# Gated mix of local attention and a spatial MLP: where w_sp is scaled, where wo is reordered, and when the late attention is issued

## The chip, the cores and the metric

The kernel runs on one core of one Trainium2 chip. A core has five engines that run their own queues of instructions: TensorE (PE, matrix products into PSUM, which has eight banks of 512 float32 columns), VectorE (DVE), ScalarE (ACT), GpSimd (POOL) and SyncE (SP). SP issues every DMA of this kernel. An engine takes its instructions strictly in order, so one that waits holds up all behind it. The metric is the device time in microseconds (us) of one execution; lower is better.

## The reference

There is one input x of 2048 rows (S) by 1024 columns (D). Two branches are computed from it and mixed by a gate per row:

```python
# A: 32 heads of 32; each position attends to 8 positions, 0, 2, 4, ... 14 back
q, k, v = split(x @ wqkv)
o = softmax(q . k[pos - 2*w] * 32**-0.5, over w = 0..7) @ v[pos - 2*w]
a = o @ wo
# B: gated MLP with a product over the positions
z = gelu(x @ w_in)                    # 2048 x 3584
z1 = z[:, :1792]
z2 = layernorm(z[:, 1792:])
g = w_sp @ z2 + b_sp[:, None]         # w_sp is 2048 x 2048
b = (z1 * g) @ w_out
# mix
s = sigmoid((x * gate_w).sum(-1))
out = s * a + (1 - s) * b
```

All inputs and the output are bfloat16.

## The kernel before, in words

Almost all of SBUF is one tile, `arena`, cut by hand into regions that are used again by later stages (`Z_OFF`, `X_OFF`, `A_OFF`, `CD_OFF`, `EF_OFF`). The instructions are written in a fixed order. A class `Beat` sets it: it counts an assumed time of TensorE (`beat.run`), and work of other engines is put into their queues when its due time in that count has come (`beat.at` for single calls, `beat.steps` for the chain of DVE work of attention). Due times decide only the order within each queue; the hardware then runs each queue as its waits allow.

The stages on TensorE, with their lines:

1. *Column chunk 0 of z2* (L274, first 128 products): x is loaded transposed, then 448 columns of the right half of `x @ w_in` are computed and passed through gelu.
2. *q/k/v* (L531): eight head groups (g) of 16 tiles; ACT copies each tile out of PSUM (L534), SP stores it to memory in three DMAs per four tiles (L540 to L542), and loads it back in another layout for attention. Attention of groups 0 to 5 runs on DVE from here on (`attention_steps`): key products (L293, L296, L299), softmax (L304 to L318, the exponential on ACT at L311), value products (L326, L332, L333, L329).
3. *The rest of z2* (L274, 384 products): gelu, sums of squares on ACT (L553), mean and variance in `stats`, normalisation to float16 in `norm`.
4. *z1* (L579): 14 column tiles f of the left half, four products of 512 rows each. ACT applies gelu (L581) into one of two slots `z1s`, and SP stores the slot to memory (L583). A slot is free again when its store has landed. All four tiles of an f, and those of the next f, find PSUM banks: there are eight.
5. *The product over positions* (L588): `g_group`, for four quarters q of the rows of w_sp and seven column pairs j. It is a Strassen-Winograd scheme with seven products instead of eight, with sums of w_sp blocks (`s_sums`) and of z2 blocks (`t_sums`) on DVE.
6. *The product with w_out* (L659): 16 row tiles in the order 8 to 15, 0 to 7; ACT scales the result into `mix` (L661). Attention of groups 6 and 7 runs on DVE beside it (`late_steps`).
7. *The product with wo* (L678, L683, L692): o, which attention stored to memory in `o_d`, is read back transposed. `combine` (L667) adds the two branches on DVE into one of three output slots, and SP stores it (L671).

Because w_sp is small in value, each of its rows is scaled by a power of two before it becomes float16. `scale_pair` does this in stage 2 for two blocks of 128 rows at a time: it loads them (L406), sums absolute values on ACT (L409), forms the power on DVE (L413, L414), scales on ACT (L419) and stores float16 rows to memory (`wsc_d`, L423). `load_half` (L445) later reads these back with transposing DMAs, four per quarter. The bias is scaled alike (`bias_scaled`), stored as `bt_d` element by element (L561) and read back broadcast to all partitions (L563). `load_wo` (L396) loads wo with a row order that fits the layout of o, by four DMAs whose destination takes every fourth partition. `load_oT_first` (L399) reads six of the eight groups of o for four row tiles; the rest (L388) and the other twelve whole row tiles (L390) are read after the late attention has stored its part (L344).

Of the kernel before, what the change touches and what calls it, by code (L numbers as in the profile page):

```python
# [11 lines left out]
BF = mybir.dt.bfloat16  # L12
# [3 lines left out]
P = 128  # L16
S = 2048
# [24 lines left out]
G_EARLY = 6  # L42
EXPO = 0x7F800000
# [14 lines left out]
def kernel(  # L58
# [31 lines left out]
    wsc_d = dpool.tile([S, S], F16, name="wsc_d")  # L90
    bt_d = dpool.tile([S], BF, name="bt_d")
    o_d = dpool.tile([S, D], BF, name="o_d")
# [33 lines left out]
    bt_n = sm.tile([P, 16], BF, name="bt_n")  # L126
    cm05 = sm.tile([P, 16], F32, name="cm05")
# [19 lines left out]
    junk = reg(EF_OFF + 3 * WGS, FH)  # L147
    w1_slots = [reg(EF_OFF + o, KT * n).rearrange("p (k c) -> p k c", k=KT)
                for o, n in ((0, 512), (4096, 512), (0, 512), (12288, 256))]
    z1s_slots = [reg(EF_OFF + 8192 + r * 2048, 2048).rearrange("p (c t) -> p c t", c=4) for r in range(2)]  # L150

    def z2_room(r, dt):
        v = reg(Z_OFF, 16 * FH) if dt is BF else reg(Z_OFF, 16 * FH).bitcast(dt)
        return v.rearrange("p (i f) -> p i f", i=16)[:, 2 * r:2 * r + 2, ZC:ZC + 1024]

    nat_slots = [z2_room(r, BF) for r in range(4)]
    sc_slots = [z2_room(4 + r, F16) for r in range(3)]
    abs_junk = z2_room(7, BF)
# [7 lines left out]
    class Half:  # L166
        def __init__(self, off):
            v = [reg(off + 2048 * r, 2048).bitcast(F16).rearrange("p (k t) -> p k t", k=8) for r in range(7)]
            both = reg(off, 8192).bitcast(F16).rearrange("p (h i t) -> p h i t", h=2, i=16)
            self.rows = [both[:, 0], both[:, 1]]  # L170
# [4 lines left out]
    y_slots = [reg(EF_OFF + r * 7168, 7168).rearrange("p (f t) -> p f t", f=NF) for r in range(2)]  # L175
    bt_bc = reg(CD_OFF + 14336, S)
    snaps = [[reg(CD_OFF + 16384 + (3 * r + n) * 512, 512).bitcast(F32) for n in range(3)] for r in range(2)]
    u3 = reg(A_OFF + 21504, 512).bitcast(F32)
    gb_slots = [reg(X_OFF + 14336 + r * 1024, 1024).rearrange("p (f t) -> p f t", f=2) for r in range(2)]

    w_out_sb = reg(CD_OFF, NF * D).rearrange("p (f n) -> p f n", f=NF)
    y_back = [reg(Z_OFF + r * 7168, 7168).rearrange("p (f t) -> p f t", f=NF) for r in range(2)]
    mix = [reg(o, 2048).bitcast(F32) for o in [Z_OFF + 14336 + 2048 * r for r in range(7)]
           + [X_OFF + 2048 * r for r in range(8)] + [EF_OFF + 8192]]
    wo_sb = reg(EF_OFF, KT * D).rearrange("p (k n) -> p k n", k=KT)
    ob_slots = [reg(CD_OFF + 16384 + r * 1024, 1024) for r in range(3)]
    oT_first = [reg(EF_OFF + 10240 + r * 768, 768).rearrange("p (k t) -> p k t", k=6) for r in range(4)]
    oT_rest = [reg(EF_OFF + 13312 + r * 256, 256).rearrange("p (k t) -> p k t", k=2) for r in range(4)]
    oT_whole = [reg(A_OFF + r * 1024, 1024).rearrange("p (k t) -> p k t", k=KT) for r in range(12)]
# [156 lines left out]
    def attention_steps(g0, g1, t):  # L346
        beat.at(t - 8.0, lambda: load_qk(g0))
        beat.at(t - 7.9, lambda: load_v(g0))
        for g in range(g0, g1):
# [7 lines left out]
            beat.at(t + (1.0 if g == g0 else 5.0), soft_exp)  # L357
# [40 lines left out]
    def load_oT_first(n):  # L398
        sync.dma_start_transpose(oT_first[n], o_d[n * P:(n + 1) * P, 0:6 * C])  # L399

    def scale_pair(n, t):
        a = 2 * n

        def load():
            for r in range(2):
                sync.dma_start(nat_slots[2 * (n % 2) + r], wsp_v[a + r])  # L406

        def norm1(r):
            nc.scalar.activation(abs_junk, nat_slots[2 * (n % 2) + r], ACT.Abs, accum_out=l1[:, a + r:a + r + 1])  # L409

        def power():
            sl = slice(a, a + 2)
            nc.vector.tensor_scalar(l1[:, sl], l1[:, sl], 2.0 ** -30, 2.0 ** -11, ALU.max, ALU.mult)  # L413
            nc.vector.tensor_scalar(rs[:, sl].bitcast(U32), l1[:, sl].bitcast(U32), EXPO, EXPO,  # L414
                                    ALU.bitwise_and, ALU.bitwise_xor)
            beat.on_vector(0.4)

        def scale(r):
            nc.scalar.activation(sc_slots[(2 * n + r) % 3], nat_slots[2 * (n % 2) + r], ACT.Copy,  # L419
                                 scale=rs[:, a + r:a + r + 1])  # L420

        def store(r):
            sync.dma_start(wsc_d[(a + r) * P:(a + r + 1) * P, :].rearrange("t (n s) -> t n s", n=2),  # L423
                           sc_slots[(2 * n + r) % 3])

        beat.at(t, load)
        beat.at(t + 6.0, lambda: norm1(0))
        beat.at(t + 8.5, lambda: norm1(1))
        beat.at(t + 11.0, power)
        beat.at(t + 17.0, lambda: scale(0))  # L430
        beat.at(t + 19.5, lambda: scale(1))
        beat.at(t + 20.0, lambda: store(0))
        beat.at(t + 22.5, lambda: store(1))

# [6 lines left out]
    def load_half(q):  # L441
        for h in range(2):
            for r in range(2):
                a = 4 * q + 2 * r + h
                sync.dma_start_transpose(halves[q % 2].rows[h][:, :, r * P:(r + 1) * P], wsc_d[a * P:(a + 1) * P, :])  # L445
# [73 lines left out]
    for n in range(8):  # L519
        scale_pair(n, beat.now + 14.0 + 16.5 * n)  # L520
# [28 lines left out]
    load_w1(1)  # L549
    for i in range(16):  # L550
        for c in range(1, 4):
            z2_tile(i, c)
        nc.scalar.activation(junk, z2[:, i, :], ACT.Square, accum_out=s2[:, i:i + 1])  # L553
        if i % 4 == 3:
            beat.at(beat.now + 6.0, lambda i=i: stats(i))
            for ii in range(i - 3, i + 1):
                beat.at(beat.now + 11.0, lambda ii=ii: norm(ii))
    beat.at(beat.now + 8.0, gates)
    beat.at(beat.now + 9.0, bias_scaled)
    bt_v = bass.AP(tensor=bt_d.tensor, offset=bt_d.offset, ap=[[1, P], [P, 16], [1, 1]])  # L560
    beat.at(beat.now + 14.0, lambda: sync.dma_start(bt_v, bt_n[:].rearrange("p (a o) -> p a o", o=1)))  # L561
    beat.at(beat.now + 24.0, lambda: load_half(0))
    beat.at(beat.now + 50.0, lambda: sync.dma_start(  # L563
        bt_bc, bass.AP(tensor=bt_d.tensor, offset=bt_d.offset, ap=[[0, P], [1, S]])))

    for f in range(NF):
        ch = f // 4
        w1 = w1_slots[ch]
        if f == 4:
            load_w1(2)  # L570
        if f == 6:
            load_w1(3)
# [3 lines left out]
        for c in range(4):  # L576
# [5 lines left out]
            beat.run(KT * 512)  # L582
        sync.dma_start(z1_d[:, :, f * 512:(f + 1) * 512].rearrange("c p t -> p c t"), z1s)  # L583
# [43 lines left out]
    for q in range(NQ):  # L627
        if q < NQ - 1:
            beat.at(beat.now + 0.5, lambda q=q: load_half(q + 1))
        else:  # L630
            beat.at(beat.now + 0.5, lambda: sync.dma_start(w_out_sb, B_w_out.rearrange("(f p) n -> p f n", p=P)))
        if q == 0:
            beat.at(beat.now + 0.6, lambda: load_z1(1, 0, NF))
        elif q < NQ - 1:
            beat.at(beat.now + 3.0, lambda q=q: spill_y(q - 1))
            beat.at(beat.now + 16.0, lambda q=q: load_z1(q + 1, 0, NF))
        for j in range(NFL):
            g_group(q, j)
            if j == 4 and q < NQ - 1:
                for fn in s_sums(q + 1):  # L640
                    fn()

    beat.steps = late_steps(beat.now + 10.0)
    for r in range(2):
        beat.at(beat.now + 3.0, lambda r=r: unspill_y(r))
# [3 lines left out]
    for n, a in enumerate(order):  # L649
        q, r = a // 4, a % 4  # L650
        y = y_slots[q % 2] if q >= 2 else y_back[q]
        if n == 8:
            beat.at(beat.now + 1.0, load_wo)
            for m in range(4):
                beat.at(beat.now + 1.5, lambda m=m: load_oT_first(m))
# [9 lines left out]
    def combine(psa, a, c0, c1):  # L665
        ob = ob_slots[a % 3]
# [3 lines left out]
    def store(a, c0, c1):  # L670
        sync.dma_start(out2[a * P:(a + 1) * P, c0:c1], ob_slots[a % 3][:, c0:c1])  # L671

    first = {}
    for a in range(4):
        for c in range(2):
            first[a, c] = psum.tile([P, 512], F32, name="psa", tag="ps")
            for kt in range(6):
                nc.tensor.matmul(first[a, c][:], oT_first[a][:, kt, :], wo_sb[:, kt, 512 * c:512 * (c + 1)],  # L678
# [50 lines left out]
```

## Time and profile before

| What | us |
|---|---|
| Median of three runs (728.46 to 729.84) | 728.98 |
| The profiled execution: its own time | 731.04 |
| The profiled execution: its span in the trace | 729.3 |
| TensorE busy in the span | 697.0 |
| VectorE busy | 501.3 |
| ScalarE busy | 311.7 |
| First product of q/k/v, of the rest of z2, of z1 | 32.84, 207.34, 280.08 |
| First product over positions, with w_out | 382.56, 553.73 |
| Last product ends, by the timeline | 726.11 |

The page gives for each group of instructions its line, engine, operation, the tiles, the number of instructions, their total busy time and mean duration, and the idle time of the engine ahead of them with what ended it. The chain that ended last is TensorE for 73% of the span. A waiting instruction is put down to the engine or DMA that came last.

### The profile page before, as it was taken

What the parts mean: (1) busy time and instruction counts of PE and PEld (TensorE: products, weight loads), DVE (VectorE), ACT (ScalarE), POOL (GpSimd) and SP (SyncE); (2) the same over time, 40 slices, a digit from 0 to 9 for tenths busy, and PEclk for the clock granted to TensorE, in tenths of its full rate; (3) what the DMA queues carried; (4) which work ended last, traced back from release to release, by engine and by line L of the source; (5) the groups of instructions that cost most, each with busy time, mean ns of one, the idle gap of its engine ahead of it and who ended that gap; (6) DMA issues with size and microseconds to landing.
All of it is one profiled execution on the core that took longest, in us unless ns stands there. A gap on an engine that the chain in (4) does not pass through costs nothing.

```text
span 729.3 us, 10622 instructions
## 1 busy us (share of the span) xinstructions
PE 697.0 (96%) x4282; PEld 469.0 (64%) x4305; DVE 501.3 (69%) x556; ACT 311.7 (43%) x588; POOL 12.1 (2%) x23
## 2 busy tenths in 40 slices
PE   8999998999799999997999999999999999995698
PEld 4588887888665554443448888888886444442243
DVE  1003859999899999995964665757557764994153
ACT  4447779787768795324332222222221232210000
POOL 1000000000000121000000000000000000000000
PEclk9999999999999999999999999999999999997989
DMA  9989998999993204799449172360508206013932
GB/s 213 210 223 258 245 286 247 293 297 264 282 277 109 84 2 141 37 123 327 138 152 194 67 216 103 87 233 1 202 2 316 106 1 159 1 55 86 202 113 74
DMA packets 189520, 117.15 MB, mean 161 GB/s; under 512 B 147872, under 2 KB 171680, under 8 KB 188448
## 3 DMA queue, kind: packets, MB, share of 16 engines
q1 hardware_dynamic: 189472, 116.49, 58.9%
q8 instruction: 33, 0.54, 0.3%
q14 instruction: 15, 0.12, 0.0%
HBM read 60.30 MB, written 40.44 MB: 138 GB/s over the span
## 4 chain that ended last, share of the span: by engine, by line
PE 73%; DVE 9%; DMA 7%; SPq 5%; ACT 4%; issue 1%; DVEq 0%; ACTq 0%
PE ps L588 23%; PE ps L531 14%; PE ps L274 13%; PE ps L579 13%; PE psa L692 5%; PE psb L659 5%; DVE arena L326 2%; SPq L390 2%; DVE arena L293 2%; DMA arena<-in_B_w_sp_dram 1%; DVE arena L296 1%; DVE arena L332 1%; ACT arena L534 1%; DMA arena<-k_d 1%; DMA arena<-in_A_wo_dram 1%
## 5 line engine op out<-in xcount | busy, mean ns | idle before, releaser
L531 PE MATMUL ps<-arena 128*128 128x384 bf16 x1024 | 168.5, 328 | 6.1 <-ACT arena L534 4.4
L588 PE MATMUL ps<-arena 128*128 128x256 f16 x1568 | 171.3, 273 | 0.0
L531 PEld LDWEIGHTS <-arena 128*128 128x128 bf16 x1024 | 147.8, 144 | 26.8 <-issue 7.9
L588 PEld LDWEIGHTS <-arena 128*128 128x128 f16 x1568 | 153.4, 98 | 18.0
L579 PE MATMUL ps<-arena 128*128 128x512 bf16 x439 | 98.2, 384 | 4.4 <-ACT arena L581 3.9
L274 PE MATMUL ps<-arena 128*128 128x448 bf16 (+1 forms) x512 | 97.4, 353 | 1.1 <-DMA arena<-in_B_w_in_dram 1.1
L659 PE MATMUL psb<-arena 128*128 128x512 bf16 x439 | 96.4, 379 | 0.5
L296 DVE TENSOR_TENSOR arena<-arena 128x4096 bf16<-128x4096 bf16 (+1 forms) x64 | 77.6, 1212 | 11.6 <-DMA arena<-in_A_wo_dram 9.7
L579 PEld LDWEIGHTS <-arena 128*128 128x128 bf16 x448 | 44.2, 99 | 58.2 <-issue 6.4
L274 PEld LDWEIGHTS <-arena 128*128 128x128 bf16 x512 | 50.0, 98 | 48.0 <-issue 1.6
L293 DVE TENSOR_TENSOR arena<-arena 128x8192 bf16<-128x8192 bf16 x16 | 70.8, 4422 | 11.1 <-DMA arena<-k_d 10.9
L659 PEld LDWEIGHTS <-arena 128*128 128x128 bf16 x448 | 43.8, 98 | 52.7
L326 DVE TENSOR_TENSOR arena<-arena,att_A 128x8192 bf16<-128x8192 bf16 x16 | 70.8, 4422 | 9.0 <-DMA arena<-v_d 8.7
L534 ACT CAST arena<-ps 128x384 bf16<-128x384 f32 x128 | 55.3, 495 | 23.6 <-PE ps L531 19.4
L581 ACT ACTIVATE arena<-ps 128x512 bf16<-128x512 f32 x56 | 32.2, 598 | 65.2 <-PE ps L579 40.3
L661 ACT ACTIVATE arena<-psb,omr 128x512 f32<-128x512 f32 x32 | 21.6, 687 | 72.2 <-PE psb L659 61.9
L667 DVE SCALAR_TENSOR_TENSOR arena<-psa,g_s,arena 128x512 bf16<-128x512 f32 (+2 forms) x33 | 23.4, 732 | 41.8 <-DMA out_dram<-arena 16.9
L692 PE MATMUL psa<-arena 128*128 128x512 bf16 (+2 forms) x197 | 44.3, 387 | 6.7 <-DVE arena L667 6.0
L606 ACT COPY arena<-ps 128x256 f32<-128x256 f32 x28 | 10.4, 372 | 84.5 <-PE ps L588 84.5
L276 ACT ACTIVATE arena<-ps 128x448 bf16<-128x448 f32 x64 | 34.3, 537 | 24.4 <-PE ps L274 23.9
L692 PEld LDWEIGHTS <-arena 128*128 128x128 bf16 x200 | 19.8, 101 | 31.6 <-issue 9.9
L615 DVE TENSOR_TENSOR arena<-ps,arena 128x256 f32<-128x256 f32 x28 | 11.9, 423 | 39.9 <-PE ps L588 39.7
(78 smaller groups left out, 479.3 us busy)
## 6 DMA issues: line engine op xcount, KB each, us to landing
arena<-z_d SPq DMA_DIRECT2D x5, 1792.0 KB, 7.5
arena<-in_B_w_sp_dram SPq DMA_DIRECT2D x16, 512.0 KB, 5.6
wsc_d<-arena SPq DMA_DIRECT2D x16, 512.0 KB, 5.6
arena<-k_d SPq DMA_DIRECT2D x8, 960.0 KB, 7.0
arena<-v_d SPq DMA_DIRECT2D x8, 960.0 KB, 7.1
z_d<-arena SPq DMA_DIRECT2D x14, 512.0 KB, 3.4
arena<-in_A_wqkv_dram SPq DMA_DIRECT2D x24, 256.0 KB, 4.7
q_d<-arena SPq DMA_DIRECT2D x32, 128.0 KB, 4.4
```

The source lines that it names most:

```text
L274: nc.tensor.matmul(ps[:, 0:N], xT[:, kt, i * P:(i + 1) * P], w2[:, kt, ZC * c:ZC * c + N], start=(kt == 0), stop=(kt == KT - 1))
L276: nc.scalar.activation(z2[:, i, ZC * c:ZC * (c + 1)], ps[:, 0:ZC], ACT.Gelu_apprx_tanh, accum_out=s1[:, 4 * i + c:4 * i + c + 1])
L293: TT(prod.rearrange("p (w j c) -> p w j c", w=W, j=8, c=C), in0, in1, ALU.mult)
L296: return lambda: TT(pv[:, :, 0:half], pv[:, :, 0:half], pv[:, :, half:2 * half], ALU.add)
L326: TT(prod.rearrange("p (w j d h) -> p w j d h", w=W, j=8, d=DH, h=HG), in0, in1, ALU.mult)
L531: nc.tensor.matmul(ps[:, 0:3 * C].rearrange("p (t c) -> p t c", t=3), lhsT, wgt[:, 0:3, kt, :], start=(kt == 0), stop=(kt == KT - 1))
L534: nc.scalar.copy(st[:, j % 4, :], ps[:, 0:3 * C])
L579: nc.tensor.matmul(ps[:], w1[:, kt, (f % 4) * P:(f % 4 + 1) * P], xT[:, kt, 512 * c:512 * (c + 1)], start=(kt == 0), stop=(kt == KT - 1))
L581: nc.scalar.activation(z1s[:, c, :], ps[:], ACT.Gelu_apprx_tanh)
L588: nc.tensor.matmul(ps[:, 0:CW], w[:, k, j * P:(j + 1) * P], v[:, k, :], start=(first and k == 0), stop=(k == 7), skip_group_check=True)
L659: nc.tensor.matmul(psb[:], y[:, f, r * P:(r + 1) * P], w_out_sb[:, f, 512 * c:512 * (c + 1)], start=(f == 0), stop=(f == NF - 1))
L692: nc.tensor.matmul(psa[:, 0:c1 - c0], oT_whole[a - 4][:, kt, :], wo_sb[:, kt, c0:c1], start=(kt == 0), stop=(kt == KT - 1))
```

## The change

It has five parts.

- *w_sp.* The float16 copy in memory is gone. `load_rows` reads rows of w_sp itself by transposing DMAs, and `scale_rows` multiplies them on DVE by their powers, which vary along the free axis now and so must be broadcast to all partitions. For that the powers are stored to memory element by element (`row_store`, into `rs_d`) and read back broadcast (`load_scale`, one per quarter). The row sums stay on ACT (`row_norm`): ten blocks of 128 rows in stage 2, with more time between load and sum, six in stage 3. There they alternate with the sums of squares, of which ten move into stage 4, with the statistics and normalisations that hang on them. `row_power` is done for ten and for six blocks at a time.
- *Regions.* What lay in `CD_OFF` and `EF_OFF` in stages 4 to 7 mostly trades places. Chunks 1 to 3 of the weights of z1 are loaded at the start of stage 4, where chunk 1 was loaded at the start of stage 3 before.
- *wo.* `order_wo` copies wo from memory to memory in its new row order in stage 3, and `load_wo` then reads it with one plain DMA.
- *Late attention.* It is put into the queues 5 us earlier by the count, and its exponentials at once after their inputs.
- *o.* Six of the eight groups of o are read transposed for all 16 row tiles during stage 6 (`load_oT_most`), and only two groups (16 small transposes) after the late attention. There are 16 output slots instead of three.

```diff
-    w1_slots = [reg(EF_OFF + o, KT * n).rearrange("p (k c) -> p k c", k=KT)
-                for o, n in ((0, 512), (4096, 512), (0, 512), (12288, 256))]
+    w1_slots = [reg(CD_OFF + o, KT * n).rearrange("p (k c) -> p k c", k=KT)
+                for o, n in ((14848, 512), (0, 512), (4096, 512), (8192, 256))]
...
-    halves = [Half(CD_OFF), Half(X_OFF)]
+    halves = [Half(EF_OFF), Half(X_OFF)]
...
+    oT_rest = [reg(A_OFF + r * 256, 256).rearrange("p (k t) -> p k t", k=2) for r in range(16)]
+    ob_slots = [reg(A_OFF + 4096 + r * 1024, 1024) for r in range(16)]
...
-            beat.at(t + (1.0 if g == g0 else 5.0), soft_exp)
+            beat.at(t + (0.0 if late else 1.0 if g == g0 else 5.0), soft_exp)
...
         yield from attention_steps(0, G_EARLY, t)
+        for h in range(2):
+            yield 0.0, 2.3, lambda h=h: scale_rows(0, h)
...
-        for n in range(4):
-            beat.at(t + 8.0, lambda n=n: sync.dma_start_transpose(oT_rest[n], o_d[n * P:(n + 1) * P, 6 * C:8 * C]))
-        for n in range(12):
-            beat.at(t + 8.5, lambda n=n: sync.dma_start_transpose(oT_whole[n], o_d[(4 + n) * P:(5 + n) * P, :]))
+        for n in range(16):
+            beat.at(t + 1.0, lambda n=n: sync.dma_start_transpose(oT_rest[n], o_d[n * P:(n + 1) * P, 6 * C:8 * C]))
+
+    def order_wo():
+        for h in range(HG):
+            sync.dma_start(wop_d.rearrange("(g d h) n -> h g d n", g=NG, d=DH, h=HG)[h],
+                           A_wo.rearrange("(g h d) n -> h g d n", g=NG, h=HG, d=DH)[h])

     def load_wo():
-        pitch = wo_sb.ap[0][0]
-        for h in range(HG):
-            dst = bass.AP(tensor=wo_sb.tensor, offset=wo_sb.offset + h * pitch, ap=[[pitch * HG, DH], [D, KT], [1, D]])
-            sync.dma_start(dst, wo_v[:, h, :, :].rearrange("g d n -> d g n"))
+        sync.dma_start(wo_sb, wop_d.rearrange("(k p) n -> p k n", p=P))
+
+    def load_oT_most(n):
+        sync.dma_start_transpose(oT_most[n], o_d[n * P:(n + 1) * P, 0:6 * C])
...
+    def row_store():
+        sync.dma_start(bass.AP(tensor=rs_d.tensor, offset=rs_d.offset, ap=[[1, P], [P, 16], [1, 1]]),
+                       rs_n[:].rearrange("p (a o) -> p a o", o=1))
...
+    def load_rows(q, h, r):
+        a = 4 * q + 2 * r + h
+        sync.dma_start_transpose(halves[q % 2].raw[h][:, :, r * P:(r + 1) * P], B_w_sp[a * P:(a + 1) * P, :])
+
+    def load_scale(q):
+        sync.dma_start(rs_bc[q % 2], bass.AP(tensor=rs_d.tensor, offset=rs_d.offset + 512 * q, ap=[[0, P], [1, 512]]))
+
+    def scale_rows(q, h):
+        v = halves[q % 2]
+        bc = _sub_ap(rs_bc[q % 2], P * h, [[0, 16], [2 * P, 2], [1, P]])
+        TT(v.scaled[h].rearrange("p i (r t) -> p i r t", r=2), v.raw[h].rearrange("p i (r t) -> p i r t", r=2),
+           bc, ALU.mult)
...
-    for n in range(8):
-        scale_pair(n, beat.now + 14.0 + 16.5 * n)
+    for n in range(L1_EARLY):
+        t = beat.now + 14.0 + 14.5 * n
+        beat.at(t, lambda n=n: load_nat(n, nat_early[n % 3]))
+        beat.at(t + 10.0, lambda n=n: row_norm(n, nat_early[n % 3], abs_junk))
...
+    load_w1(1)
+    t = beat.now
+    beat.at(t + 3.0, lambda: row_power(L1_EARLY, 16))
+    beat.at(t + 6.0, row_store)
...
+    beat.at(t + 14.0, lambda: sync.dma_start(bt_v, bt_n[:].rearrange("p (a o) -> p a o", o=1)))
+    beat.at(t + 16.0, lambda: load_scale(0))
...
-        if f == 4:
+        if f == 1:
             load_w1(2)
-        if f == 6:
+        if f == 2:
             load_w1(3)
...
+            if square[0] < 16 and (c == 3 or (c == 1 and f % 2 == 1)):
+                squares()
...
-            if j == 4 and q < NQ - 1:
-                for fn in s_sums(q + 1):
-                    fn()
-
-    beat.steps = late_steps(beat.now + 10.0)
+            if q < NQ - 1:
+                if j in (2, 3):
+                    scale_rows(q + 1, j - 2)
+                elif j in (4, 5):
+                    for fn in s_sums(q + 1)[2 * (j - 4):2 * (j - 3)]:
+                        fn()
+
+    beat.steps = late_steps(beat.now + 5.0)
...
+    for n in range(5):
+        beat.at(beat.now + 12.0, lambda n=n: load_oT_most(n))
...
-        ob = ob_slots[a % 3]
+        ob = ob_slots[a]
```

More of the change, by code (lines that the diff above doesn't have):

```diff
@@ L89 @@
     z1_d = dpool.tile([NQ, P, NF * 512], BF, name="z1_d")
-    wsc_d = dpool.tile([S, S], F16, name="wsc_d")
+    rs_d = dpool.tile([S], BF, name="rs_d")
     bt_d = dpool.tile([S], BF, name="bt_d")
+    wop_d = dpool.tile([D, D], BF, name="wop_d")
     o_d = dpool.tile([S, D], BF, name="o_d")
@@ L185 @@
[L185 to L189, printed above, removed]
+           + [X_OFF + 2048 * r for r in range(8)] + [CD_OFF + 14336]]
@@ L346, in attention_steps @@
     def attention_steps(g0, g1, t):
+        late = g0 > 0
         beat.at(t - 8.0, lambda: load_qk(g0))
@@ L398, in load_oT_first @@
[L398 to L433, printed above, removed]
@@ L548, with squares @@
     load_w1(0)
-    load_w1(1)
+    load_nat(L1_EARLY, nat_late[0])
+    t = beat.now
+    for n in range(4):
+        beat.at(t + 6.0 + 15.0 * n, lambda n=n: load_rows(0, n // 2, n % 2))
+    beat.at(t + 40.0, order_wo)
+    beat.at(t + 3.0, lambda: row_power(0, L1_EARLY))
+    square = [0]
+    def squares():
+        i = square[0]
+        square[0] += 1
+        nc.scalar.activation(junk[:, 0:FH], z2[:, i, :], ACT.Square, accum_out=s2[:, i:i + 1])
+        if i % 4 == 3:
+            beat.at(beat.now + 4.0, lambda i=i: stats(i))
+            for ii in range(i - 3, i + 1):
+                beat.at(beat.now + 8.0, lambda ii=ii: norm(ii))
     for i in range(16):
@@ L677 @@
             for kt in range(6):
-                nc.tensor.matmul(first[a, c][:], oT_first[a][:, kt, :], wo_sb[:, kt, 512 * c:512 * (c + 1)],
+                nc.tensor.matmul(first[a, c][:], oT_most[a][:, kt, :], wo_sb[:, kt, 512 * c:512 * (c + 1)],
                                  start=(kt == 0), stop=False)
@@ L691 @@
             for kt in range(KT):
-                nc.tensor.matmul(psa[:, 0:c1 - c0], oT_whole[a - 4][:, kt, :], wo_sb[:, kt, c0:c1],
-                                 start=(kt == 0), stop=(kt == KT - 1))
+                lhsT = oT_most[a][:, kt, :] if kt < 6 else oT_rest[a][:, kt - 6, :]
+                nc.tensor.matmul(psa[:, 0:c1 - c0], lhsT, wo_sb[:, kt, c0:c1], start=(kt == 0), stop=(kt == KT - 1))
             combine(psa, a, c0, c1)
```

93 lines of the change are left out of this document (57 added, 36 removed).

## The prediction, made before the changed kernel was run

> **What bounds the kernel now.** I read the page's busy row first: TensorE (PE) is busy 697.0 of 729.3 us, so only its idle time, and the slow clock after it, can be won. The view of waits for PE says where that is (us in total, times, longest):
>
> ```profile
> PE psa L683 <- DMA arena<-o_d: 8.4, 1, 8.4
> PE psa L692 <- DVE arena L667: 6.0, 1, 6.0
> PE ps L531 <- ACT arena L534: 4.4, 3, 3.8
> PE ps L579 <- ACT arena L581: 3.9, 1, 3.9
> PE ps L531 <- ACT arena L252: 1.7, 1, 1.7
> ```
>
> Two waits lie in the last stage, one in the z1 stage (L579), the others in the q/k/v stage (L531). Each gap also costs clock. The first 2 us with work after the z1 gap (columns: us, length, busy and count of PE, PEld, DVE, ACT, POOL, granted clock, DMA share, GB/s):
>
> ```profile
> 332.00:334.00 2.00, 1.64 (x4) 0.55 (x4) 0.00 (x0) 1.78 (x4) 0.00 (x0) 0.60 0.93 262
> ```
>
> Then the timelines around those gaps (start and length in us; in brackets the idle time before and what ended it). SP, which issues every DMA:
>
> ```profile
> 300.11 0.36 SPq L561 DMA_DIRECT2D bt_d<-bt_n  x1
> 301.52 0.36 SPq L583 DMA_DIRECT2D z_d<-arena  x1
> 301.97 25.80 SPq L445 DMA_TRANSPOSE arena<-wsc_d  x4
> ```
>
> DMA issues from 298 to 302 us, with KB and us to landing:
>
> ```profile
> z_d<-arena SPq DMA_DIRECT2D x1, 512.0 KB, 18.0
> bt_d<-bt_n SPq DMA_DIRECT2D x1, 4.0 KB, 18.4
> ```
>
> ScalarE (ACT), then VectorE (DVE):
>
> ```profile
> 319.64 1.57 ACT L581 ACTIVATE arena<-ps 128x512 bf16<-128x512 f32 x3 [11.24 <-DMA z_d<-arena]
> 331.72 2.07 ACT L581 ACTIVATE arena<-ps 128x512 bf16<-128x512 f32 x4 [6.65 <-DMA z_d<-arena]
> ```
>
> ```profile
> 589.67 0.43 DVE L314 TENSOR_TENSOR att_m<-att_L 128x256 f32<-128x256 f32 x1 [10.14 <-ACT att_L L311]
> 616.10 4.93 DVE L296 TENSOR_TENSOR arena<-arena 128x4096 bf16<-128x4096 bf16 x4 [9.68 <-DMA arena<-in_A_wo_dram]
> 660.68 0.69 DVE L329 TENSOR_TENSOR arena<-arena 128x1024 bf16<-128x1024 bf16 x1
> ```
>
> The reader should see: a 4 KB store of 2048 separate 2-byte elements takes 18.4 us, and the 512 KB z1 store issued 1.4 us behind it lands at 319.5 us, just after it (median of such stores: 3.4). ACT stood 11.2 us for that store's slot; the eight PSUM banks covered it. At the end, late attention closes at 661.4 us, after two holes of 10.14 and 9.68 us.
>
> **The change, part by part** (all times on the profiled execution's clock: span 729.3, its time 731.04; the median of the runs shown is 728.98, so I take the difference off the median).
>
> *Last stage.* PE runs from 553.73 to 726.11. Its 448 products of L659 take 96.5 us (to 650.26), so 0.2155 each; the whole stage is 704 such (448+48+16+192), 151.7 us. So 20.7 us of it is loss: the waits 8.4+0.2+0.6+6.0 and 5.5 of slow clock. Does it all go? The exponential of head group 6 now stands behind the 9th eviction of L661, not the 11th (queue of the changed kernel as built); evictions come 3.02 us apart, so 6.05 us less. The second hole is a DMA to `wo_sb` whose destination steps over partitions; DVE and ACT both wait for it though they touch other columns. The plain load from `wop_d` should make nobody wait: 9.68 less. Attention then ends at 661.4-6.05-9.68 = 645.6. The second exponential (19th eviction, done 611.8) still falls in the 17.4 us of group 6's value products. The last v load follows eight oT transposes on SP, at most 2.04 us each (8.17 for 4 at L399) from 602, so it is issued when its buffer is free (621.6) and needed 6.5 us later, which it kept before (637.31 to 643.86). Storing o takes 5.4 us (661.40 to 666.80): 651.0. Then 16 transposes of 256 columns, at most 1.27 us each (5.06 for 4 at L388), 2.33 to land: the fourth is there at 657. PE needs the first at 650.26+10.5 = 660.8, then one per 3.45 us: 4 us of slack. Sixteen `ob_slots` remove the 6.0. I take 20.4; ends 20.7 (all of the loss) and 6 (only the output-slot wait gone).
>
> *q/k/v stage.* The stage takes 174.5 us (32.84 to 207.34); at 31.21 us per 192 products it would be 166.5. Sixteen stores of 512 KB and six loads leave it, with 16 ACT scalings of 2.03, and ten norms now come 10 us after their loads. I take 7.5 of the 8.0; ends 2 and 8. The z1 stage would start at 272.6 instead of 280.1.
>
> *z2 stage.* ACT per row block: three gelus 0.73, a copy 0.15 and either a square (1.89) or a norm (2.11): at most 4.45 against PE's 4.55, and four blocks have neither. DVE loses nothing. Nothing on PE's path: 0. The two rs powers are 0.2 us each; `order_wo`, nat loads and row transposes run where the DMA share is 0.13 to 0.22: 0.
>
> *z1 stage, the price.* SP now queues: rs store (2048 elements, as bt), z1 store f=0, w1 chunk 2, store f=1, chunk 3, bt store, scale load (waits for the rs store to land), store f=2, f=3, v load. The rs store waits for the second `row_power`, which stands inside group 5's key products on DVE. DVE's chain: group 1 started at 100.94; its waits of 6.83 and 1.90 shrink (no norm waiting for DMA ahead of the exponential), I take 95. From 100.94 to 284.54, where group 5's key products began, lie four blocks of one head group: 183.6 us, less 16.0 of waits, norms and powers, so 41.9 each. Three blocks, 39.7 us to the end of the next value products, then stats 0.9, soft_b 2.3, key products 4.5, norms 2.7, rest 5.6+4.5+2.3, powers 1.0: 284.3. So rs lands at 302.7. Behind it 2.5 MB at some 330 GB/s (seen after 328 us): 7.8. Then bt, which nothing before shows queued behind another: 0 to 18.4, I take 18.4-1, since the z1 store kept behind bt. Then the store of f=2, issued when f=0's slot came free at 304, lands at about 330. Eight banks let PE go eight tiles ahead: f=4 waits for f=2's first eviction, f=6 for f=4's, which needs f=2's store. So f=6 starts at 330.3 (272.6+41.4 = 314.0 without waits), a stall of 16 in two pieces, plus 2.3 of slow clock (before: 50 products took 12.85 for 10.8). Before, f=6 started at 280.1+41.4+3.9+2.0 = 327.5. Net of both stages: +5.1. QKV's gain is swallowed here, because DVE sets this time, not PE. Ends: -7 (no queueing) and +12.
>
> The Trainium skill, "DMA: Bandwidth & Descriptors", section "Queues, rings and completion order", says each DMA engine takes descriptors of one issuing engine in ring order; by that the two element stores add up and the sum is the one above; by overlap it would be 17 less. The same page, section "Rules for kernel authors", says that an access whose last dimension isn't contiguous becomes one descriptor per element and should be rearranged, which speaks against a second store of this kind; the trace agrees for the one before (18.4 us for 4 KB), and no row shows two in a row.
>
> *Scaling on DVE* (128x4096, four columns of the page's groups: 2.29 for L296, all bf16; 4.42 for twice the columns): 2.29 to 4.42 each; the nearest row is 2.29, same width. Two in the z1 chain (4.6), two per product stage at j=2, 3: there a group has 6.1 us and DVE 3.5 of work, and four sums in one group (4.9) made no gap. 0. The Trainium skill, "VectorE: DVE Perf Modes", section "What auto-detection actually checks", lets a two-input operation take two elements a cycle where every tensor is 16-bit with step one; by that the lower end holds, and the sum is the same by either.
>
> *DVE at the first product.* The v load lands behind bt, about 335; value products 17.4, stats and norm 3.6, scaling 4.6, sums 4.9 and 15.5: 381 (385). PE ends z1 at 330.3+55.2+2.3 = 387.8. Cover of 3 to 7 us: 0.
>
> **Sum:** -20.4+5.1 = -15.3. 728.98-15.3 = 713.7, say 714.
>
> **The rivals.** (1) *The second element store costs the ring nothing:* only the first piece of the stall stays, 272.6+27.6 = 300.2 to 304.2, and 2 of clock. z1 ends at 272.6+96.7+6 = 375.3 instead of 382.6; DVE, its v load in time, at about 370. -20.4-7.3 = 27.7 less: 701. Against: the 18.0 of the z1 store behind bt; for: data of other transfers moved while bt ran (16 to 42 GB/s in the 2 us windows from 310 to 316). (2) *The tail keeps its first wait:* if the holes on DVE only move (the wait on the wo load is not its partition step, and the last v load comes late), o arrives at 666.8 as before; 8.4 and 2.2 of slow clock stay, so 10 are won instead of 20.4: 724. One hole alone costs 3 (o at 660.7, first columns at 663 for 660.8) and stays in the forecast. For it: I infer the cause of the 9.68 from the code, the view names only the DMA. (3) *Slower, by one mechanism:* the rs store runs with 2.5 MB queued around it, and an element store then costs more than 18.4 (143 ns for each of an engine's 128 elements, if 16 share them). The stall takes both, so from (15.3+1.5)/2 = 8.4 us more each, 26.8, the kernel is slower; at 30 each, 737. For: it is the only DMA of its kind, seen once; against: 0.9 MB already moved beside it. (4) *The change doesn't do what it says:* the built queues show the exponentials, loads and transposes where described, so this is only (2).
>
> **How the numbers follow.** Forecast 0.60 (705 to 721), rival 1 0.13, rival 2 0.12, slower 0.12, no change 0.03; 0.2% (1.5 us) is what measurement can tell. Faster 0.85, same 0.03, slower 0.12. Range 700 to 727: it takes in rivals 1 and 2 and leaves out all that is not faster (0.15).
>
> **What would show it.** Right: no PE wait at L683/L692's lines but one or two of 4 and 12 us in z1, on ACT, which waits for z1 stores of 20 us or more; DVE's wait on wo gone; no scaled wsc traffic in q/k/v. Wrong: z1 stalls above 25 or below 6; a DVE wait at the first product; PE still waiting for o.

## The result, and the profile after

The changed kernel takes 715.71 us (median of four runs, 715.23 to 716.1). The kernel before, run on the same chip beside it, takes 728.72. The ratio is 0.982, with a 95% interval from 0.9803 to 0.9837. The profiled execution took 715.23 us, its span is 713.5. The prediction was 714, in a range from 700 to 727. Single executions in a slower state of the chip are left out of all times and ratios here (one, of the kernel before at 1042.15 us, beside the last experiment).

The timelines of TensorE (PE) cut both spans into stages. A stage begins with its first product; the numbers are us.

| Stage | before | after | difference | predicted |
|---|---|---|---|---|
| q/k/v | 174.5 | 166.4 | -8.1 | -7.5 |
| rest of z2 | 72.75 | 72.75 | 0 | 0 |
| z1 | 102.5 | 115.3 | +12.8 | +12.6 |
| product over positions | 171.2 | 171.2 | 0 | 0 |
| w_out and wo | 172.5 | 152.1 | -20.4 | -20.4 |
| whole span | 729.3 | 713.5 | -15.8 | -15.3 |

(The predicted +12.6 is the net of +5.1 of two stages plus the 7.5 won in q/k/v.)

The view of waits for PE, of the kernel after (us in total, times, longest). Of the five waits that headed it before, one is left, and it has grown from 3.9 to 14.8 us:

```profile
PE ps L604 <- ACT arena L606: 14.8, 2, 8.7
PE pw L102 <- DVE warm L97: 1.2, 1, 1.2
```

PE's timeline, first in the z1 stage, then at the end:

```profile
305.54 15.84 PE L604 MATMUL ps<-arena 128*128 128x512 bf16 x63 [6.14 <-ACT arena L606]
330.07 56.97 PE L604 MATMUL ps<-arena 128*128 128x512 bf16 x251 [8.69 <-ACT arena L606]
...
654.74 10.52 PE L716 MATMUL psa<-arena 128*128 128x512 bf16 x47
665.10 3.62 PE L721 MATMUL psa<-arena 128*128 128x512 bf16 x15
668.55 41.62 PE L731 MATMUL psa<-arena 128*128 128x512 bf16 x197
```

The last three rows carry no bracket, which means that PE did not wait ahead of them: at the end of the kernel it waits for nothing. The z1 rows show the two predicted pieces of stall. What ACT waited for there, and the two DMAs that stand in the chain that ended last (start, us, what):

```profile
304.89 1.58 ACT L606 ACTIVATE arena<-ps 128x512 bf16<-128x512 f32 x3 [17.00 <-DMA z_d<-arena]
329.42 2.06 ACT L606 ACTIVATE arena<-ps 128x512 bf16<-128x512 f32 x4 [12.12 <-DMA z_d<-arena]
```

```profile
285.55 19.27 DMA z_d<-arena
...
310.35 18.99 DMA z_d<-arena
```

Each is a 512 KB store of a z1 slot, and the page's median for such a store is 2.9 us. SP's timeline shows what each one stood behind:

```profile
285.08 0.38 SPq L425 DMA_DIRECT2D rs_d<-rs_n  x1
285.55 0.80 SPq L610 DMA_DIRECT2D z_d<-arena  x1
...
288.54 12.57 SPq L479 DMA_DIRECT2D arena<-in_B_w_in_dram  x1
301.21 4.52 SPq L586 DMA_DIRECT2D bt_d<-bt_n  x1
...
310.35 5.66 SPq L610 DMA_DIRECT2D z_d<-arena  x2
```

The first is queued behind the 4 KB element store of the powers (`rs_d`), the second behind that of the bias (`bt_d`). The stalls also cost clock. In the table of 2 us windows (columns as in the prediction) the granted clock, third number from the end, is 0.50 and 0.66 after the first stall and 0.50 after the second, instead of 1.00:

```profile
306.00:308.00 2.00, 2.00 (x6) 0.66 (x5) 1.97 (x2) 1.97 (x3) 0.00 (x0) 0.50 1.09 369
308.00:310.00 2.00, 2.00 (x8) 0.75 (x7) 2.00 (x1) 1.97 (x3) 0.00 (x0) 0.66 1.25 238
310.00:312.00 2.00, 2.00 (x11) 0.94 (x10) 1.93 (x3) 2.00 (x4) 0.00 (x0) 1.00 0.15 1
...
330.00:332.00 2.00, 1.93 (x5) 0.69 (x5) 0.00 (x0) 2.00 (x5) 0.00 (x0) 0.50 0.73 305
```

Five to eight products lie in 2 us there, and eleven at full clock. VectorE (DVE) shows the other new or removed pieces: a scaling of two blocks, the exponential's wait in late attention, and attention's last instruction:

```profile
354.16 4.49 DVE L444 TENSOR_TENSOR arena<-arena 128x4096 f16<-128x4096 bf16 x2
...
588.10 0.42 DVE L320 TENSOR_TENSOR att_m<-att_L 128x256 f32<-128x256 f32 x1 [4.89 <-ACT att_L L317]
...
649.46 0.69 DVE L335 TENSOR_TENSOR arena<-arena 128x1024 bf16<-128x1024 bf16 x1
```

The wait for wo is gone. Attention ends 92.1 us after the first w_out product (650.15 - 558.05), where it ended 107.8 us after it before (661.37 - 553.57).

### The profile page after: what moved, and what is told of

Read it like the earlier page. It is cut to its first block, busy times and chain, and to the rows that moved or that the text cites. A ratio compares the mean times of both kernels' runs of the same rounds, so it can differ in the third digit from the quotient of the medians.

```text
span 713.5 us, 10625 instructions
## 1 busy us (share of the span) xinstructions
PE 692.1 (97%) x4282; PEld 468.3 (66%) x4305; DVE 517.5 (73%) x554; ACT 284.7 (40%) x572; POOL 8.8 (1%) x23
## 4 chain that ended last, share of the span: by engine, by line
PE 92%; DMA 6%; ACT 1%; issue 0%; SPq 0%; DVE 0%; DVEq 0%; ACTq 0%
PE ps L615 24%; PE ps L533 23%; PE psb L697 13%; PE ps L280 13%; PE ps L604 10%; PE psa L731 6%; DMA z_d<-arena 5%; PE psa L716 1%; DMA arena<-in_A_x_dram 1%; PE psa L721 0%; ACT arena L606 0%; PE pt L267 0%; ACT L317 0%; ACT att_L L317 0%; DVE arena L705 0%
## 5 line engine op out<-in xcount | busy, mean ns | idle before, releaser
L533 PE MATMUL ps<-arena 128*128 128x384 bf16 x1024 | 166.6, 326 | 0.0
L604 PE MATMUL ps<-arena 128*128 128x512 bf16 x439 | 100.1, 388 | 15.3 <-ACT arena L606 14.8
L536 ACT CAST arena<-ps 128x384 bf16<-128x384 f32 x128 | 59.5, 482 | 73.0 <-PE ps L533 69.6
L302 DVE TENSOR_TENSOR arena<-arena 128x4096 bf16<-128x4096 bf16 (+1 forms) x64 | 77.6, 1213 | 2.1
L705 DVE SCALAR_TENSOR_TENSOR arena<-psa,g_s,arena 128x512 bf16<-128x512 f32 (+2 forms) x33 | 23.4, 733 | 37.1 <-PE psa L731 20.5
L731 PE MATMUL psa<-arena 128*128 128x512 bf16 (+2 forms) x197 | 41.5, 370 | 0.2
L338 DVE TENSOR_TENSOR arena<-arena 128x4096 bf16<-128x4096 bf16 x16 | 36.7, 2291 | 0.5
```

The costliest lines, as they stand in the source:

```text
L302: return lambda: TT(pv[:, :, 0:half], pv[:, :, 0:half], pv[:, :, half:2 * half], ALU.add)
L338: return [(4.4, mul), (2.3, lambda: TT(p3[:, 0:4, :], p3[:, 0:4, :], p3[:, 4:8, :], ALU.add)), (1.2, lambda: TT(p3[:, 0:2, :], p3[:, 0:2, ...
L533: nc.tensor.matmul(ps[:, 0:3 * C].rearrange("p (t c) -> p t c", t=3), lhsT, wgt[:, 0:3, kt, :], start=(kt == 0), stop=(kt == KT - 1))
L536: nc.scalar.copy(st[:, j % 4, :], ps[:, 0:3 * C])
L604: nc.tensor.matmul(ps[:], w1[:, kt, (f % 4) * P:(f % 4 + 1) * P], xT[:, kt, 512 * c:512 * (c + 1)], start=(kt == 0), stop=(kt == KT - 1))
L731: nc.tensor.matmul(psa[:, 0:c1 - c0], lhsT, wo_sb[:, kt, c0:c1], start=(kt == 0), stop=(kt == KT - 1))
```

## The experiments

The time of the kernel before differs a little from one set of runs to the next (728.61, 730.87, 728.4), so kernels are compared by their ratio to it.

**The two halves.** Two kernels split the change. The first is the kernel before with the changes to wo, the late attention, the reading of o and the output slots; w_sp is handled as before. Its core:

```diff
-            sync.dma_start(dst, wo_v[:, h, :, :].rearrange("g d n -> d g n"))
+        sync.dma_start(wo_sb, wop_d.rearrange("(k p) n -> p k n", p=P))
...
+    beat.at(beat.now + 40.0, order_wo)
...
-            beat.at(t + (1.0 if g == g0 else 5.0), soft_exp)
+            beat.at(t + (0.0 if late else 1.0 if g == g0 else 5.0), soft_exp)
...
-        for n in range(12):
-            beat.at(t + 8.5, lambda n=n: sync.dma_start_transpose(oT_whole[n], o_d[(4 + n) * P:(5 + n) * P, :]))
+        for n in range(16):
+            beat.at(t + 1.0, lambda n=n: sync.dma_start_transpose(oT_rest[n], o_d[n * P:(n + 1) * P, 6 * C:8 * C]))
...
-        ob = ob_slots[a % 3]
+        ob = ob_slots[a]
```

> The kernel before with the last two parts of the change alone (wo reordered in memory, late attention sooner, o transposed early, 16 output slots). Theory: the tail's gain needs nothing of the w_sp part. From the first product with w_out to the last product the changed kernel takes 151.5 us and the kernel before 172.4, so 20.8 less: 708. Rival: part of it leans on the lighter queues of the w_sp part; then 711 to 722.

Measured: 708.61 us, ratio 0.9734 (0.9711 to 0.9757). This half alone wins more than the whole change. Its last stage has no PE wait; the largest waits that are left are those of the q/k/v and z1 stages of before:

```profile
PE ps L534 <- ACT arena L537: 5.2, 2, 4.1
PE ps L583 <- ACT arena L585: 3.3, 1, 3.3
```

The second is the changed kernel with the last stages of before (the same diff the other way round).

> The changed kernel with the last stages of the kernel before (wo loaded over partition steps, late attention as before, o read back late, three output slots). Theory: what is left, the w_sp part, costs more in z1 than it wins in q/k/v. The first product with w_out comes at 558.21 us in the changed kernel and at 553.73 before, so 4.5 slower than before: 733. Rival: the w_sp part wins by itself (8 us in q/k/v) and the stall is an effect of both parts together: 721 to 727.

Measured: 735.29 us, ratio 1.0062 (1.0036 to 1.0088), so slower, by 4.4 us against the 730.87 beside it. Its waits hold the z1 stall of the kernel after and both end waits of the kernel before:

```profile
PE ps L600 <- ACT arena L602: 15.5, 2, 8.2
PE psa L712 <- DMA arena<-o_d: 7.6, 1, 7.6
PE psa L721 <- DVE arena L696: 6.3, 1, 6.3
```

The two effects, -2.66% and +0.62%, add to -2.04%; the whole change measured -1.8%, a difference that the three intervals cover. So the new handling of w_sp, with all that it takes out of q/k/v, is a net loss as it stands.

**Whose is the z1 stall?** Two kernels avoid element stores. A column of 128x16 values is turned into 16 rows of 256 bytes by one TensorE transpose and one ACT copy, and these rows are stored. In the first, both the powers and the bias are treated so. The two stores also go into the queue later, with f=4, and the read of the powers with them:

```diff
+    def store_rows(n, src, dst):
+        pt = psum.tile([P, 4, P], BF, name="pt", tag="ps")
+        nc.tensor.transpose(pt[0:16, 0, :], src[:], ident[:])
+        nc.scalar.copy(rowsT[0:16, n * P:(n + 1) * P], pt[0:16, 0, :])
+        sync.dma_start(dst.rearrange("(a t) -> a t", t=P), rowsT[0:16, n * P:(n + 1) * P])
...
-    beat.at(t + 6.0, row_store)
-    beat.at(t + 14.0, lambda: sync.dma_start(bt_v, bt_n[:].rearrange("p (a o) -> p a o", o=1)))
-    beat.at(t + 16.0, lambda: load_scale(0))
+    beat.at(t + 40.0, lambda: load_scale(0))
...
+        if f == 4:
+            store_rows(0, rs_n, rs_d)
+            store_rows(1, bt_n, bt_d)
```

> The changed kernel, with the powers and the scaled bias turned by one small TensorE transpose each (128x16 to 16x128) and stored as 16 rows of 256 bytes, so that no store of single elements is left. Theory (the two element stores one behind the other hold the z1 stores): both stalls of the z1 stage, 6.1 and 8.7 us, go with some 4 of slow clock; PE would end z1 at 271.8+96.7 = 368.5 instead of 387.0, and DVE's chain, about 366, is just early enough: 18.5 less, 697. Rival (the stalls come from what else moved into z1: the sums of squares on ACT, 1.5 MB of weights, the wait of SP for the scale load): 711 or more.

Measured: 697.31 us, ratio 0.9574 (0.956 to 0.9588), and no PE wait in z1. The second kernel does this for the powers only; the bias keeps its element store, at its old due time.

> The changed kernel, with only the powers stored as 16 rows; the bias stays an element store. Theory: one element store alone is covered by the eight PSUM banks, as it was in the kernel before (ACT waited 11.2 us, PE 0 for that cause): no stall, 697 to 700. Rival (each element store costs a stall of its own size): half of the stall stays, 706 to 709. Rival (other causes): 711 or more.

Measured: 697.21 us, ratio 0.9571 (0.9557 to 0.9586): no different from both. Here is what SP did, and ACT's only long wait for a slot:

```profile
279.31 0.38 SPq L618 DMA_DIRECT2D z_d<-arena  x1
...
291.02 0.37 SPq L592 DMA_DIRECT2D bt_d<-bt_n  x1
```

```profile
311.70 2.06 ACT L614 ACTIVATE arena<-ps 128x512 bf16<-128x512 f32 x4 [9.40 <-DMA z_d<-arena]
```

The bias store is as dear as ever (18.3 us to land), and ACT still waits 9.4 us for a z1 slot, but PE doesn't: its banks cover this. One element store is not what stalls PE; something about two, or about the place of the first, is.

So the next kernel keeps both element stores and puts the second far from the first:

```diff
-    beat.at(t + 14.0, lambda: sync.dma_start(bt_v, bt_n[:].rearrange("p (a o) -> p a o", o=1)))
+    beat.at(t + 55.0, lambda: sync.dma_start(bt_v, bt_n[:].rearrange("p (a o) -> p a o", o=1)))
...
-    beat.at(t + 50.0, lambda: sync.dma_start(
+    beat.at(t + 85.0, lambda: sync.dma_start(
```

> The changed kernel, with the element store of the bias put 41 us later into the queues and its load 35 us later; no work is taken away. Theory (it is the two in a row that makes the second stall): the first stall of 6.1 stays, the second goes with its slow clock, 715.7-8.7-2.3 = 705, at most 708 if the late store meets a bad moment. Rival (each costs its own stall wherever it stands): 715.

Measured: 705.4 us, ratio 0.9683 (0.9667 to 0.9699), as the theory had it. PE's timeline in z1, and ACT's wait behind the late bias store:

```profile
271.87 27.79 PE L604 MATMUL ps<-arena 128*128 128x512 bf16 x125
306.50 70.64 PE L604 MATMUL ps<-arena 128*128 128x512 bf16 x314 [6.84 <-ACT arena L606]
```

```profile
350.06 2.07 ACT L606 ACTIVATE arena<-ps 128x512 bf16<-128x512 f32 x4 [6.77 <-DMA z_d<-arena]
```

The second piece of stall is gone and the bias store is covered again. But the store of the powers, now alone, still stalls PE for 6.84 us, while in the run before the bias store alone stalled it for none. The difference lies on SP's queue. Without the store of the powers, SP issued the z1 store of f=0 at 279.31. With it, SP stood waiting for `row_power` until 285.08, with that z1 store behind it, and issued it at 285.55.

In the kernel with the late bias store, the times of that one z1 store add up to the stall. ACT began the last part of the slot of f=0 at 278.97:

```profile
278.97 0.60 ACT L606 ACTIVATE arena<-ps 128x512 bf16<-128x512 f32 x1 [1.13 <-PE ps L604]
```

The store itself stands in the chain that ended last, at 285.77 with 20.00 us. So the slot was full at 279.6, and PE found free banks until 299.7 (271.87 + 27.79), which is a cover of 20.1 us. The store first stood 6.2 us on SP and then took 20.0 us, 6.1 us more than the cover. With 0.7 us for ACT's next tile, that makes the 6.8 us of the stall. Issued when it was ready, even a store of 20.0 us would have just been covered; this is an estimate from these rows.

The last kernel tests this by order alone. It queues the store of the powers behind the first two z1 stores and takes no work away. The two loads of weights then stand ahead of it too, and the read of the powers follows it later:

```diff
-    beat.at(t + 6.0, row_store)
+    beat.at(t + 16.0, row_store)
...
-    beat.at(t + 14.0, lambda: sync.dma_start(bt_v, bt_n[:].rearrange("p (a o) -> p a o", o=1)))
-    beat.at(t + 16.0, lambda: load_scale(0))
-    beat.at(t + 50.0, lambda: sync.dma_start(
+    beat.at(t + 55.0, lambda: sync.dma_start(bt_v, bt_n[:].rearrange("p (a o) -> p a o", o=1)))
+    beat.at(t + 36.0, lambda: load_scale(0))
+    beat.at(t + 85.0, lambda: sync.dma_start(
```

> The changed kernel, with the store of the first layer's column scales (two bytes at a time, as it is) queued on SP ten steps later, behind the z1 stores of f = 0 and f = 1 and the loads of w1's chunks 2 and 3, and the loads and stores that follow it moved later in the same order. No work is taken away and no transfer gets cheaper. Theory: the one stall of 6.8 us that was left with the bias store late came about because the z1 store of f = 0, ready at about 280 us, stood on SP behind the wait for row_power until 285 and then 19.3 us behind the element store on the ring. With that store ahead of it the stage has two to three rounds of its three buffers in hand, and TensorE waits for nothing in it: 0 us in place of 6.8, the half clock around the stall gone, 697 to 699 us. Rival: the first element store costs its stall wherever it stands, since what is queued behind it, z1 stores or others, is held 19 us against a cover of 20 us or less: one stall of 5 to 8 us, and 704 to 707 us.

Measured: 696.74 us, ratio 0.957 (0.9551 to 0.9589). PE's largest waits, its whole z1 stage in one row, and SP's queue:

```profile
PE pw L102 <- DVE warm L97: 1.2, 1, 1.2
PE ps L280 <- DMA arena<-in_B_w_in_dram: 0.9, 1, 0.9
```

```profile
271.64 96.86 PE L604 MATMUL ps<-arena 128*128 128x512 bf16 x448
```

```profile
279.37 0.38 SPq L610 DMA_DIRECT2D z_d<-arena  x1
279.84 0.46 SPq L479 DMA_DIRECT2D arena<-in_B_w_in_dram  x1
286.27 0.37 SPq L610 DMA_DIRECT2D z_d<-arena  x1
286.73 0.46 SPq L479 DMA_DIRECT2D arena<-in_B_w_in_dram  x1
287.29 1.14 SPq L425 DMA_DIRECT2D rs_d<-rs_n  x1
295.31 5.67 SPq L610 DMA_DIRECT2D z_d<-arena  x2
...
321.22 0.50 SPq L586 DMA_DIRECT2D bt_d<-bt_n  x1
```

Both element stores are there, and what stands behind them still waits: the z1 store issued at 295.31 took 12.7 us to land, the one issued at 327.71 took 13.3. PE waits for neither. The rival, that the first element store costs its stall wherever it stands, is out. This is the fastest kernel of the study, level with the two that store rows: 4.3% under the kernel before, where the change as made is 1.8% under it, and the difference is the due times of four calls.

**The end, part by part.** Three kernels each take one piece of the end back out of the changed kernel. First the plain load of wo (the old partition-stepped load, no `order_wo`):

```diff
     def load_wo():
-        sync.dma_start(wo_sb, wop_d.rearrange("(k p) n -> p k n", p=P))
+        pitch = wo_sb.ap[0][0]
+        for h in range(HG):
+            dst = bass.AP(tensor=wo_sb.tensor, offset=wo_sb.offset + h * pitch, ap=[[pitch * HG, DH], [D, KT], [1, D]])
+            sync.dma_start(dst, A_wo.rearrange("(g h d) n -> h d g n", g=NG, h=HG, d=DH)[h])
```

> The changed kernel with the old load of wo (four DMAs whose destination steps over partitions) and without the copy in memory. Theory (that destination makes DVE and ACT wait though they touch other columns): the hole of 9.68 us on DVE comes back, attention ends 9.7 later, the first columns of o land at about 668 where PE needs them at 665.1: 3 us of wait and 1 to 2 of slow clock, 719 to 721. Rival (the hole came from the traffic of wo or from what stood around it before): 716.

Measured: 720.43 us, ratio 0.9872 (0.9843 to 0.9901). DVE's hole is back on the first key sum after the load, and PE waits for o again:

```profile
619.20 0.62 DVE L302 TENSOR_TENSOR arena<-arena 128x512 bf16<-128x512 bf16 x1 [10.20 <-DMA arena<-in_A_wo_dram]
```

```profile
PE psa L723 <- DMA arena<-o_d: 2.8, 1, 2.8
```

By the code DVE touches nothing of `wo_sb` there. In the changed kernel the plain load of the same 2 MB, issued at 604.00, moves its data until about 612, and DVE does the same four sums meanwhile without a wait:

```profile
604.88 4.94 DVE L302 TENSOR_TENSOR arena<-arena 128x4096 bf16<-128x4096 bf16 x4
```

So the wait comes with the old form of the load, as the prediction inferred. That form has four transfers, source rows that are taken in another order and a destination that steps over partitions; which of these brings the wait was not separated. It costs 10.2 us on DVE and, after slack, 3.8 us of time (0.52% by the ratios). SP's waits show that the hold goes both ways: SP stood 33.0 us ahead of the old load for a key sum of DVE (L302) and 1.1 us more for ACT, and issued it at 610.18. The plain load went out at 604.00 and waited only for PE. An order that makes each side wait for the other, though by the code they touch different columns, looks like one that the program sets, and not like traffic. No run tests this.

Then three output slots instead of sixteen:

```diff
-        ob = ob_slots[a]
+        ob = ob_slots[a % 3]
```

> The changed kernel with three output slots instead of sixteen. Theory as in the prediction (the slots remove PE's wait of 6.0): it comes back with 2 of slow clock, 722 to 724. Rival (the wait before came from whole-tile transposes holding SP until 688; now SP is free at 676.5, 11 us after the first output, and eight PSUM banks cover the rest): 716.

Measured: 716.65 us, ratio 0.9815 (0.9795 to 0.9834). Against the 0.982 of the changed kernel that is no difference, so the theory of the prediction (6 us, 722 to 724) fell. DVE does wait for an output store, but PE hardly does:

```profile
679.16 5.36 DVE L705 SCALAR_TENSOR_TENSOR arena<-psa,g_s,arena 128x512 bf16<-128x512 f32 x8 [9.11 <-DMA out_dram<-arena]
```

```profile
PE psa L731 <- DVE arena L705: 0.6, 1, 0.6
```

What lay behind PE's 6.0 us of before is to be seen in SP's timeline of before. Output stores stood behind twelve whole-tile transposes until 688.41, with DVE waiting 16.26 us for the first of them:

```profile
671.91 16.40 SPq L390 DMA_TRANSPOSE arena<-o_d  x12
688.41 21.56 SPq L671 DMA_DIRECT2D out_dram<-arena  x11
```

With o read mostly early, the 16 small transposes end 11.6 us earlier, at 676.8, in this kernel too. So with o read early the thirteen further slots are worth nothing. Whether sixteen slots would have removed the wait with o read late was not run.

Last, the late attention at its old due times:

```diff
-            beat.at(t + (0.0 if late else 1.0 if g == g0 else 5.0), soft_exp)
+            beat.at(t + (1.0 if g == g0 else 5.0), soft_exp)
...
-    beat.steps = late_steps(beat.now + 5.0)
+    beat.steps = late_steps(beat.now + 10.0)
```

> The changed kernel with the late attention and its exponentials put into the queues as late as before. Theory: attention ends 6.05 us later (2 evictions), the first columns of o land at 664.3 and PE needs them at 665.1, so the 6.05 us were slack and the time stays: 716, at most 717. Rival (no slack as PE's first wait in the kernel before would have it): 721.

Measured: 715.4 us, ratio 0.9798 (0.9777 to 0.9819), the same as the changed kernel within the intervals. DVE's wait for the exponential is back in full, and no PE wait comes of it:

```profile
594.54 0.43 DVE L320 TENSOR_TENSOR att_m<-att_L 128x256 f32<-128x256 f32 x1 [10.94 <-ACT att_L L317]
```

The 16 transposes start at 661.96 instead of 655.98; PE needs the first at 665.50. The 6 us are all slack, once wo is out of the way.

Taken back one by one, these three parts cost 3.8 us, nothing and nothing. The early reading of o was not taken back by itself, so its share of the 20.4 us is read from SP's timelines and not measured.

## Why the prediction was right, step by step

- **q/k/v.** -7.5 taken, -8.1 measured, and the split confirms whose it is: the w_sp half alone has the 166.4 us, the other half alone stays at 175.5 (33.02 to 208.47). PE has no wait left in the stage. "ends 2 and 8": the upper end came. Which of the pieces that left the stage wins the time, no run separates.
- **z2.** 0 taken, 0 measured (72.75 both), with six row sums of w_sp more on ACT and ten sums of squares less.
- **When the store of the powers can start.** DVE's chain to the second `row_power` was put at 284.3. SP issued the store at 285.08. Group 1's key products started at 94.9 for 95.
- **The stall.** "a stall of 16 in two pieces", f=6 at 330.3: measured 6.14 + 8.69 = 14.83 and 330.07. The chain shows two z1 stores, each held 19 us behind an element store, as described. The Trainium skill ("DMA: Bandwidth & Descriptors", section "Queues, rings and completion order") has each DMA engine take the descriptors of one issuing engine in ring order; the trace agrees for these two stores, with 19.27 and 18.99 us in place of 2.9. The two element stores add up as well, but not in the way that the prediction had it: SP issued the second only at 301.21, 16.1 us behind the first (285.08). In the kernel with the late bias store, the first had landed 19.6 us after its issue, when SP had waited for it (285.31 to 304.92). So the two can have been in flight together for about 3.5 us only, and what two that are issued close together do, on which the first rival (701) turns, was not seen.
- **Luck in that term.** The bias store landed at 323.8 (301.21 + 22.6), where 327.9 was taken (310.5 + 17.4); the z1 store behind it landed 5.5 us after that, where 2 were taken. The stall came out 1.2 us short and the slow clock 1.6 us long. These misses nearly cancel. One reading was wrong without effect on the sum: the wait of before lay ahead of f=7 and not of f=6, since PE ran 48.5 us of z1 ahead of it (224 products at 0.2155 are 48.3).
- **Slow clock.** 2.3 taken; 115.26 - 14.83 - 96.5 (448 products at 0.2155) = 3.9 measured, since each of the two pieces was long enough to bring it. The Trainium skill ("TensorE: Matmul & The Clock Gate", section "What's actually happening") puts the halving after an idle window of about 3.4 us; the rows agree, with 0.50 after the idle times of 6.1 and 8.7 us.
- **Scaling on DVE.** 2.29 taken, 2.25 (4.49 for two) and 2.28 to 2.29 measured: with bfloat16 in and float16 out it is as fast as the rows with bfloat16 alone (2.29), the lower end. DVE was done at 378.8 (predicted 381), PE at 386.87 (387.8): a cover of 8 us where 3 to 7 was expected.
- **The end.** 20.4 taken, 20.4 measured. Attention ended 15.7 us earlier after the stage's start, as summed (6.05 + 9.68). The transposes started 5.8 us after the store of o was issued (5.4 taken), 20.5 us for 16 (20.3 taken at most). PE needed the first at 665.1, and they had started at 656.0. The slack was put at 4 us; the kernel with the old due times used up 6 without a wait of PE.

Two steps of the end name a cause that the runs do not bear out. *"Sixteen `ob_slots` remove the 6.0"*: the wait is gone with three slots too, as long as o is read early. The wait was put down to the slot because DVE's wait named a store to `out_dram`; what held that store was one step further back, on SP. *The 6.05 us of the earlier exponentials*, summed into 20.4, bought slack and no time. With the wo hole still open they may be worth something: PE waits 2.8 us for o with that hole alone, and 7.6 us in the w_sp half, which has the hole, the late exponentials and the late reading of o. No run has the first two alone.

One step was incomplete. The price of the first piece of stall was ascribed to the element store alone. The runs show that it takes two things: 19 to 20 us behind the store, and a z1 store that had been ready for some 6 us while SP waited for DVE. The prediction named SP's queue order and the wait for `row_power`, but not what that wait did to the z1 store behind it; with the z1 store ahead of it, the piece costs nothing.

The gain of the q/k/v stage went into that stall: in the kernel with the later store, z1 takes 96.7 us (271.64 to 368.33) where after the change it takes 115.3, and its 18.6 us are the whole distance from 713.5 to 694.9 of span. DVE is then done at 364.9, 3.5 us before the first product over positions; so little more can be won ahead of that product without a faster chain on DVE.

## What to carry to other kernels

Before a wait is put into a queue that also issues stores, look at what is ready behind it. Here a store whose data came from a slow chain on DVE, queued 10 us too early by the count, cost 8.7 of the 18.6 us (span 703.6 against 694.9) by holding back a finished store, and moving it needed no cheaper transfer. A long element store was harmless here while what queued behind it had enough buffers in hand, so place it where its followers are furthest from their need, and if two are needed, keep them apart. And when a wait names a buffer that is not free, follow the transfer that would free it back to its issue before adding buffers.

## What the runs showed of the hardware that was not expected

SP itself can be held in issuing. Behind the element store of the powers, and with a z1 store, 1 MB of weights and another z1 store queued as well, the issue of one more load (512 KB of weights) took 12.57 us, where it takes 0.46 elsewhere; with the bias store later, it took 13.31. In the kernels in which the loads of weights stand ahead of the element store, the same issue takes 0.46. So the bias store was issued at 301.21, though its values were ready at about 291 and the kernel that stores only the powers as rows issued it at 291.02. The prediction did not have this wait; it changed little in the sum, because the prediction had the bias store start its work only behind the same transfers. Whether it is the amount of transfers outstanding that holds SP was not tried, and stays open.
